# A query tile's ratio moves to GpSimd (a power of minus one and a product), and the first half of the steps stands in another order

## The chip, the cores and the metric

The kernel runs on one core of a Trainium2 chip. The core has five engines that each work through their own list of instructions in order and wait for one another by semaphores: TensorE (PE in the profile; its weight loads are shown as PEld), VectorE (DVE), ScalarE (ACT), GpSimd (POOL) and SyncE (SP), whose queue issues the DMAs here. The metric is the device time of one execution in microseconds, as the median of several runs. Before the change it is 237.27 us (three runs, 236.63 to 237.54).

## The reference, cut to what matters

One transformer block over 2048 tokens of width 640, in bf16: linear attention with a learned feature map, and a feed forward unit, each behind a layer norm and with a residual.

```
q, k, v = split(layernorm(x) @ wqkv)          # 32 heads of 20
pq = q @ w_phi ; pk = k @ w_phi               # per head, 20 x 20
phi_q = concat(softmax(pq), softmax(-pq))     # 40 features per head
phi_k = concat(softmax(pk), softmax(-pk))
kv = phi_k^T v ; z = sum over tokens of phi_k
o  = (phi_q kv) / (phi_q z + 1e-6)
h  = x + o @ wo
out = h + silu(layernorm(h) @ w1) @ w2        # 640 -> 1728 -> 640
```

Since `o` is a quotient, a common factor of a head's 40 query features falls out, but the ratio of the two softmax halves does not. So for the queries the kernel needs only, for each token and head, the ratio of the two sums of exponentials: sum(exp(pq)) / sum(exp(-pq)). The second half of the features is multiplied by it.

## The kernel before

The 2048 tokens are 16 tiles of 128 rows, t = 0 to 15. The kernel is a set of named steps, and a list written out by hand, ORDER, says in which order their instructions are issued. An engine's own list is therefore ORDER, cut down to that engine. The table ON says on which engine some of the steps run.

The steps that this document speaks of, by name (the number is the tile):

- `st`, `rs`, `xn`, `xt`: mean and variance of a row of x (`moments`, VectorE), the inverse deviation (`inv_std`: on GpSimd as an addition of eps and a power of -0.5, on ScalarE as a Ln and an Exp), the normalised tile, and its transposition into XnT (by DMA from SP's queue from tile 4 on).
- `wq`, `phq`, `fq`, `fqe`: w_phi is folded into the query weights: transposed loads into WTq, a block diagonal phi_q, the product, and its copy into Wfq. `wk` and `fk` do the same for the keys.
- `K`, `ex`, `su`, `rk`, `sc`, `V`, `ve`, `kv`: keys and values of a tile on TensorE, exponentials on ScalarE, sums and scaling on VectorE, and the sum over tokens kv. `bd` makes the block diagonal KVB from it.
- `Q`, `qe`, `qs`, `qr`, `qt`: the queries on TensorE, the two exponentials EQ (ScalarE), their sums Sq (VectorE, `query_sums`), the ratio and the scaling of EQ's second half (VectorE, `query_ratio`), and the transposition into EqT by DMA.
- `D`, `E`, `ot`, `G`, `ga`: phi_q kv on TensorE, the division on VectorE, the transposition of O, the product with wo, and the residual into X on VectorE.
- `ls`, `lr`, `hn`, `ht`: the second layer norm: moments (VectorE), `inv_std` (GpSimd), the normalised tile (VectorE), and its transposition into HnT by DMA.
- `u`, `s`, `d`, `oa`, `out`: the feed forward in units of tiles (0,1), (2 to 5), (6 to 9), (10 to 13) and (14,15). `u2.8` is the piece of unit 2 that starts at slice 8 of the 1728 features, `s2.8` its Silu on ScalarE, written into shT; `uA.L`, `sA.L`, `lt` are the last half slice. `d60` is the product with w2 for tile 6, first half of the columns; it reads all 13 slices of its unit's shT one after the other. `oa` adds the residual (VectorE), `out` stores.

From the step `halves` on, TensorE's results go round a ring of eight banks (`ps_half`): a step takes the bank that was taken eight takings earlier, and waits until that one has been read.

Around the change: `u2.2` is the first step of the second feed forward unit and reads HnT of tiles 2 to 5 at once. The lines that the texts speak of are 435 to 444 (`inv_std`), 432 and 433 (`moments`), 448 (`normal`), 660 (`query_sums`), 668 to 680 (`query_ratio`), 709 (`attend`), 721 and 722 (`divide`), 742 and 749 (`out_projection`, `residual`), 824 and 844 (`ffn_up`, `ffn_silu`), 864 (`ffn_down`) and 873 (`ffn_out`). In the changed kernel the same lines stand 5 to 9 further down.

Of the kernel before, what the change touches and what calls it, by code (L numbers as in the profile page):

```python
# [31 lines left out]
ve14 qt1 load0 rk14 ex15 qe2 kv12 sc14 load1 su15 V15 kv13 rk15 ve15 Q3 qs2 kv14 load9 sc15 kv15 qr2 Q5
Q7 bd1 bd0 qe3 qe5 halves D0 qs3 Q4 qt2 E00 E01 qe7 qe4 qr3 D1 Q6 E10 Q9 E11 Q8 qe6 qe9 qs4 qr4 qs5 Q10
ot0 qr5 qt3 Q11 ot1 qe8 qe10 D2 qe11 E20 G00 G01 ga00 E21 D3 E30 qt4 E31 ga01 G10 ga10 ot2 G11 ga11 Q14
Q12 qe14 ot3 ls0 D4 lr0 G20 Q13 ls1 G30 qe12 lr1 hn0 qt5 E40 G21 G31 hn1 E41 ht0 ht1 ga30 ga20 qs6 Q15
qe13 pad1 ga21 D5 ga31 qs7 qr6 u0.0 E50 u0.6 qe15 E51 ls3 qr7 ls2 s0.0 load8 u0.L s0.L s0.6 u0.10 ot4
u0.12 u0.8 lr3 G40 G41 lr2 s0.12 s0.10 u0.4 load10 hn3 qt6 ga41 ot5 ga40 u0.2 s0.8 ls4 D6 lt0 G50 qt7
E60 lr4 G51 E61 ht3 ga51 s0.2 s0.4 d10 D7 ga50 hn4 ls5 ot6 lr5 hn2 qs8 d00 E70 hn5 oa00 ht2 d01 G60 ht4
G61 qr8 oa10 d11 ht5 ga61 u2.2 u2.0 ga60 qt8 E71 ot7 s2.0 oa01 qs9 u2.L qs13 s2.2 qr9 oa11 qs11 u2.6 D8
u2.10 E80 ls6 qt9 u2.7 u2.3 s2.L u2.11 s2.10 s2.6 qr13 E81 u2.9 s2.9 qr11 u2.5 qs12 s2.7 qs10 s2.3 u2.1  # L40
D9 G70 s2.5 E90 qr10 u2.12 s2.11 E91 ot8 G71 u2.4 lr6 ga71 ga70 qt11 out0 lt2 s2.1 qt10 u2.8 out1 hn6
s2.4 qr12 ls7 G80 s2.8 ga80 ot9 G81 D11 s2.12 E110 d30 ht6 qt13 E111 d20 D10 ga81 lr7 G90 E100 oa30 oa20
E101 ot10 G91 hn7 ga91 d31 ot11 ga90 ls8 qs15 lr8 d21 qt12 oa31 d50 G100 ls9 G101 hn8 out3 d40 d51 ht8
lr9 hn9 oa21 ga101 G110 out2 ga100 ga110 oa50 oa40 G111 qs14 d41 oa51 D12 ls10 ht7 E120 ht9 u6.1 u6.0
oa41 ga111 u6.12 u6.8 D13 s6.0 s6.1 qr14 s6.8 E121 s6.12 u6.11 ot12 u6.2 u6.3 qr15 lr10 s6.11 u6.L s6.2
E130 ls11 out4 E131 u6.9 qt15 s6.3 G120 ot13 s6.L u6.6 lt6 s6.6 lr11 u6.7 u6.10 hn10 u6.5 out5 s6.7 hn11
s6.9 u6.4 qt14 G121 ga120 ga121 s6.5 ht11 G130 D14 G131 E140 ga131 s6.10 s6.4 d60 ls12 oa60 d61 d70 ht10
lr12 E141 d91 ga130 ls13 oa61 hn12 oa70 D15 lr13 d90 ht12 ot14 d71 hn13 ht13 out6 G140 oa71 oa90 u10.L
oa91 ga140 out9 E150 u10.0 u10.1 out7 E151 u10.6 G141 u10.9 s10.L s10.0 s10.6 u10.8 ga141 d80 u10.7
s10.1 u10.3 u10.11 ot15 s10.3 u10.5 u10.12 oa80 s10.9 s10.8 s10.11 u10.2 u10.4 ls14 s10.7 s10.5 u10.10  # L50
s10.12 s10.4 G150 G151 lt10 lr14 d81 s10.10 s10.2 d110 hn14 oa81 ht14 out8 d111 ga150 d120 ga151 ls15
# [7 lines left out]
def kernel(  # L59
# [23 lines left out]
    HC = 3  # L83
# [14 lines left out]
    persist = ctx.enter_context(tc.tile_pool(name="persist", bufs=1))  # L98
# [6 lines left out]
    pools = {"att": None, "late": None}  # L105
# [24 lines left out]
    def ps_half_bf16():  # L130
# [66 lines left out]
    mask = persist.tile([P, SPLIT, HC, HV], F32, name="mask")  # L197
# [12 lines left out]
    def add(name, emit):  # L210
        steps[name] = emit
# [450 lines left out]
    def query_ratio(t):  # L664
        n = HC * NCH
        s3 = sq.pop(t)[:].rearrange("p c (h b) -> p (c h) b", b=2)
        rm = pools["att"].tile([P, n], F32, name="Rq")
        nc.vector.reciprocal(rm[:], s3[:, :, 1])
        r2 = pools["att"].tile([P, n, 2], BF16, name="Rho")
        nc.vector.tensor_tensor(  # L670
            r2[:],
            s3[:, :, 0].unsqueeze(2).to_broadcast([P, n, 2]),
            rm[:].unsqueeze(2).to_broadcast([P, n, 2]),
            op=ALU.mult,
        )
        Em = features(t, 0, NCH)[:, :, :, 1].rearrange("p c h (f e) -> p c h f e", e=2)
        r5 = r2[:].rearrange("p (c h) e -> p c h e", h=HC)
        nc.vector.tensor_tensor(
            Em, Em, r5.unsqueeze(3).to_broadcast([P, NCH, HC, DH // 2, 2]), op=ALU.mult
        )  # L680
# [105 lines left out]
    for t in range(T):  # L786
# [154 lines left out]
```

## Time and profile before

| | |
|---|---|
| median of three runs | 237.27 us (236.63 to 237.54) |
| the profiled execution | 236.82 us |
| its span, first to last instruction | 234.8 us |
| TensorE busy | 229.5 us, 98% of the span, 1984 matmuls |
| VectorE busy | 165.8 us, 71%, 349 instructions |
| ScalarE busy | 105.1 us, 45%, 222 instructions |
| GpSimd busy | 64.4 us, 27%, 103 instructions |
| granted TensorE clock | 0.999 |

How to read it. L668 is line 668 of the kernel before. A row of the groups gives line, engine, operation, tile written <- tiles read, shapes, count | busy time in all (us), mean of one (ns) | idle time of the engine just before them, and what ended it. A row of the timeline gives the start (us), the time it took, engine, line, operation and, in brackets, idle time before it and what released it. A row of the waits gives who waited for whom: us in total, times, longest. The chain is the work that ended last, followed back to the start; its rows are start, time, engine and line. TensorE's matmuls are pipelined: the row of one is longer than its share of the time, which is read from a row of many. SPq is the issuing of DMAs.

### The profile page before, as it was taken

How to read it: one execution, taken by the hardware profiler on the slowest of the kernel's cores; microseconds unless marked ns; L12 is line 12 of the kernel's file. 1: busy time of each engine (PE TensorE's matmuls, PEld its weight loads, DVE VectorE, ACT ScalarE, POOL GpSimd, SP SyncE). 2: the span in 40 equal slices, each digit the busy share in tenths (PEclk: the TensorE clock that was granted, in tenths of full speed). 3: DMA queues.
4: the chain of work that ended last, by engine and by line, in shares of the span. 5: the costliest groups of instructions: out<-in, count | busy, mean ns of one | idle time of the engine just before them, and what ended most of it. 6: DMA issues, size and time to landing. Idle time of an engine off the chain costs nothing.

```text
span 234.8 us, 5031 instructions
## 1 busy us (share of the span) xinstructions
PE 229.5 (98%) x1984; PEld 161.2 (69%) x1984; DVE 165.8 (71%) x349; ACT 105.1 (45%) x222; POOL 64.4 (27%) x103
## 2 busy tenths in 40 slices
PE   8999989999999999999999999999999999999995
PEld 6777767777777777887545777645677455778874
DVE  3999979999999999999999795792472330404031
ACT  3999979877969754610234100054300326001410
POOL 5699999996000020121010111011020010100000
PEclk9999999999999999999999999999999999999999
DMA  6995379668976749694325946127313301011011
GB/s 165 346 228 138 88 162 149 181 59 172 245 270 73 155 94 159 148 120 95 81 64 133 163 97 173 31 56 176 72 24 88 98 0 28 30 29 56 8 56 56
DMA packets 67213, 26.79 MB, mean 114 GB/s; under 512 B 60151, under 2 KB 66167, under 8 KB 67063
## 3 DMA queue, kind: packets, MB, share of 16 engines
q1 hardware_dynamic: 66535, 26.47, 52.9%
q8 instruction: 15, 0.25, 0.5%
q10 hardware_dynamic: 656, 0.03, 0.2%
q14 instruction: 7, 0.06, 0.1%
HBM read 9.64 MB, written 2.62 MB: 52 GB/s over the span
## 4 chain that ended last, share of the span: by engine, by line
PE 87%; DVE 5%; DMA 3%; ACT 2%; issue 1%; POOL 1%; SPq 0%; DVEq 0%; POOLq 0%
PE banks L864 24%; PE banks L824 24%; PE banks L496 16%; PE banks L742 7%; PE banks L534 4%; PE banks L587 2%; PE banks L215 2%; PE banks L867 2%; PE banks L709 2%; DMA HnT<-xn 2%; DMA WTq<-in_A_wqkv_dram 1%; DVE Sq L660 1%; ACT Wfk L323 1%; PE banks L835 1%; DVE O L722 1%
## 5 line engine op out<-in xcount | busy, mean ns | idle before, releaser
L844 ACT ACTIVATE shT<-banks 128x512 bf16<-128x512 f32 (+1 forms) x53 | 28.7, 591 | 83.2 <-PE banks L824 83.2
L864 PE MATMUL banks<-w_sb,shT 128*128 128x320 bf16 (+2 forms) x429 | 61.3, 295 | 0.0
L824 PE MATMUL banks<-HnT,w_sb 128*128 128x512 bf16 (+1 forms) x325 | 59.0, 336 | 0.5 <-DMA HnT<-xn 0.5
L864 PEld LDWEIGHTS <-shT 128*128 128x128 bf16 x429 | 41.1, 98 | 15.2
L824 PEld LDWEIGHTS <-w_sb 128*128 128x128 bf16 x325 | 31.1, 98 | 22.8 <-issue 0.6
L441 POOL TENSOR_SCALAR rs<-mv 128x1 f32<-128x1 f32 x26 | 7.7, 298 | 137.1 <-DVE mv L433 136.9
L873 DVE TENSOR_TENSOR o_t<-banks,X 128x320 bf16<-128x320 f32 (+2 forms) x33 | 14.9, 474 | 39.6 <-PE banks L867 26.7
L496 PEld LDWEIGHTS <-XnT 128*128 128x128 bf16 x300 | 28.2, 98 | 10.5 <-DMA XnT<-xn 0.4
L448 POOL TENSOR_SCALAR xn<-X,mv,rs 128x640 bf16<-128x640 bf16 x12 | 31.0, 2586 | 0.4
L432 DVE BATCH_NORM_STATS2 st<-X 128x6 f32<-128x320 bf16 x64 | 27.9, 477 | 3.3 <-DMA X<-in_A_x_dram 3.2
L656 ACT ACTIVATE EQ<-banks 128x360 bf16<-128x360 f32 (+2 forms) x52 | 22.0, 514 | 8.4 <-PE banks L534 8.2
L742 PE MATMUL banks<-wo_sb,OT 128*128 128x320 bf16 x160 | 24.8, 299 | 0.0
L660 DVE TENSOR_REDUCE Sq<-EQ 128x66 f32<-128x1320 bf16 x16 | 24.1, 1517 | 0.0
L534 PE MATMUL banks<-Wfq,XnT 128*128 128x360 bf16 (+2 forms) x160 | 23.5, 299 | 0.0
L749 DVE TENSOR_TENSOR X<-banks,X 128x320 bf16<-128x320 f32 x32 | 14.5, 483 | 12.6 <-PE banks L742 12.5
L555 DVE TENSOR_REDUCE Sk<-EK 128x64 f32<-128x1280 bf16 x16 | 23.3, 1464 | 0.2
L551 ACT ACTIVATE EK<-banks 128x640 bf16<-128x640 f32 x32 | 20.8, 701 | 4.4 <-PE banks L496 2.0
L496 PE MATMUL banks<-Wfk,XnT 128*128 128x320 bf16 x150 | 22.5, 299 | 0.0
L496 PE MATMUL banks<-Wv,XnT 128*128 128x320 bf16 x150 | 21.8, 299 | 0.0
L742 PEld LDWEIGHTS <-OT 128*128 128x128 bf16 x160 | 15.1, 98 | 6.5
L534 PEld LDWEIGHTS <-XnT 128*128 128x128 bf16 x160 | 15.1, 97 | 6.2
L444 POOL TENSOR_TENSOR rs<-rs,nhalf_t 128x1 f32<-128x1 f32 x26 | 15.9, 613 | 2.2
(71 smaller groups left out, 203.9 us busy)
## 6 DMA issues: line engine op xcount, KB each, us to landing
out_dram<-o_t SPq DMA_DIRECT2D x15, 160.0 KB, 2.0
w_sb<-in_B_w_dram SPq DMA_DIRECT2D x5, 432.0 KB, 3.9
w_sb<-in_B_w_dram SPq DMA_DIRECT2D x3, 480.0 KB, 4.5
X<-in_A_x_dram SPq DMA_DIRECT2D x1, 1280.0 KB, 7.3
Wk<-in_A_wqkv_dram SPq DMA_DIRECT2D x5, 160.0 KB, 3.5
Wv<-in_A_wqkv_dram SPq DMA_DIRECT2D x5, 160.0 KB, 5.7
wo_sb<-in_A_wo_dram SPq DMA_DIRECT2D x1, 800.0 KB, 5.7
X<-in_A_x_dram SPq DMA_DIRECT2D x1, 640.0 KB, 5.9
```

The source lines that it names most:

```text
L432: nc.vector.bn_stats(st[:, i, :], X[:, t, i * HD : (i + 1) * HD])
L448: eng.tensor_scalar(out=xn_[t][:], in0=X[:, t, :], scalar1=mv_.pop(t)[:, 0:1], scalar2=rs_.pop(t)[:], op0=ALU.subtract, op1=ALU.mult,)
L496: nc.tensor.matmul(ps[:, g, 0:HD], XnT[:, c, t * P : (t + 1) * P], W[:, c, g * HD : (g + 1) * HD], start=(c == 0), stop=(c == C - 1),)
L534: nc.tensor.matmul(ps[:, 0 : e - a], XnT[:, c, t * P : (t + 1) * P], Wfq[:, c, a:e], start=(c == 0), stop=(c == C - 1),)
L551: nc.scalar.activation(E5[:, :, :, b, :], p4, AF.Exp, scale=sign)
L555: nc.vector.tensor_reduce(sk[t][:], ek[t][:, 0 : H * HF].rearrange("p (q f) -> p q f", f=DH), axis=AX.X, op=ALU.add)
L656: nc.scalar.activation(features(t, a, b)[:, :, :, i], p4, AF.Exp, scale=sign)
L660: nc.vector.tensor_reduce(sq[t][:], EQ[0][:, t, :, 0:FCH].rearrange("p c (q f) -> p c q f", f=DH), axis=AX.X, op=ALU.add)
L742: nc.tensor.matmul(ps[:, 0:HD], ot[t][:, c, :], wo_sb[:, c, g * HD : (g + 1) * HD], start=(c == 0), stop=(c == C - 1),)
L824: nc.tensor.matmul(ps[:, at : at + n], w1_sb[:, c, fc * P : fc * P + P], HnT[u][:, c, 0:n], start=(c == 0), stop=(c == C - 1),)
L844: nc.scalar.activation(shT[u][:, f0 * n : f1 * n], ps_of.pop(("u", u, f0))[:, 0 : (f1 - f0) * n], AF.Silu)
L864: nc.tensor.matmul(ps[:, 0 : b - a], shT[u][:, at : at + P], w2_sb[:, fc, a:b], start=(fc == 0), stop=False,)
```

## The change

Three things, in one edit.

1. The ratio of a query tile is split off from the scaling. It was a reciprocal and a product on VectorE, in `qr`. It is now a step of its own, `qi`, on GpSimd: a power of minus one over 128x33 sums, and a product into 128x66, whose tile Rho has three buffers. `qr` keeps the scaling. A constant tile of minus ones is set at the start.
2. ORDER is written anew from a place behind `V0.1` up to `u2.2`; from there on only the `qi` are put in, each right ahead of its `qr`.
3. ON has other engines for some of the first layer norm's steps, and entries for the second's `lr`: tiles 0, 1, 4, 5, 7, 10 and 14 on ScalarE, the others on GpSimd as before. ON also gives `fq5e` to VectorE, and xn6 and xn11 to VectorE in place of GpSimd.

```
         n = HC * NCH
         s3 = sq.pop(t)[:].rearrange("p c (h b) -> p (c h) b", b=2)
         rm = pools["att"].tile([P, n], F32, name="Rq")
-        nc.vector.reciprocal(rm[:], s3[:, :, 1])
-        r2 = pools["att"].tile([P, n, 2], BF16, name="Rho")
-        nc.vector.tensor_tensor(
-            r2[:],
+        nc.gpsimd.tensor_tensor(rm[:], s3[:, :, 1], minus_t[:].to_broadcast([P, n]), op=ALU.pow)
+        rho[t] = pools["att"].tile([P, n, 2], BF16, name="Rho", bufs=3)
+        nc.gpsimd.tensor_tensor(
+            rho[t][:],
             s3[:, :, 0].unsqueeze(2).to_broadcast([P, n, 2]),
             rm[:].unsqueeze(2).to_broadcast([P, n, 2]),
             op=ALU.mult,
         )
+
+    def query_scale(t):
         Em = features(t, 0, NCH)[:, :, :, 1].rearrange("p c h (f e) -> p c h f e", e=2)
-        r5 = r2[:].rearrange("p (c h) e -> p c h e", h=HC)
+        r5 = rho.pop(t)[:].rearrange("p (c h) e -> p c h e", h=HC)
         nc.vector.tensor_tensor(
             Em, Em, r5.unsqueeze(3).to_broadcast([P, NCH, HC, DH // 2, 2]), op=ALU.mult
         )
...
-        add(f"qr{t}", lambda t=t: query_ratio(t))
+        add(f"qi{t}", lambda t=t: query_ratio(t))
+        add(f"qr{t}", lambda t=t: query_scale(t))
...
-        add(f"lr{t}", lambda t=t: inv_std(t))
+        eng = on(f"lr{t}", "POOL")
+        add(f"lr{t}", lambda t=t, eng=eng: inv_std(t, eng))
...
     ON = dict(
...
-        rs6="ACT", x3="ACT", xn6="POOL", rs7="POOL", xn7="POOL", fq2e="ACT", rs8="ACT", rs9="ACT",
+        rs7="ACT", xn6="DVE", rs5="POOL", xn5="DVE", xn7="POOL", fq2e="ACT", rs11="POOL", rs8="POOL",
...
+        xn15="POOL", rs14="POOL", xn14="POOL", lr0="ACT", lr1="ACT", lr2="POOL", lr3="POOL", lr5="ACT",
+        lr4="ACT", lr6="POOL", lr7="ACT", lr8="POOL", lr9="POOL", lr10="ACT", lr11="POOL", lr12="POOL",
+        lr13="POOL", lr14="ACT", lr15="POOL",
```

Places of the new ORDER that the texts name:

```
after V0.1:   V0.4 pad0 x2 su0 xt3 ex1 rk0 ones7 st7 x3 K2 ex2 ve0 su1 rs6 rs7 wq3 st5 wph0 xn6 V1 V2 V3
              ve1 rk1 rs5 sc0 X8 ve2 ve3 phq xn5 ones3 K3 kv0 st9 xt4 sc1 V4 su2 fq2 wq0 ...
before u2.2:  ... u0.6 s0.4 D6 lt0 G40 E60 u0.12 qt7 s0.12 G50 G51 lr2 hn2 ga40 ls3 s0.6 lr3 E61 ga51
              ga50 G41 ot6 ls5 ga41 qi8 d10 hn3 d00 lr5 ls4 hn5 lr4 D7 ht2 ht3 G60 hn4 oa00 ht5 G61 d01
              d11 qr8 E70 ga61 ht4 oa10 u2.2
lr7:          ... s2.12 E110 d30 ht6 qt13 E111 d20 D10 ga81 lr7 G90 E100 oa30 oa20 E101 ot10 G91 hn7
lr10:         u6.1 u6.0 oa41 ga111 u6.12 u6.8 D13 s6.0 s6.1 qi14 qr14 s6.8 E121 s6.12 u6.11 ot12 u6.2
              u6.3 qi15 qr15 lr10 s6.11 u6.L s6.2 E130 ls11 out4 E131 u6.9 qt15 s6.3 G120 ... u6.6 ...
              u6.7 u6.10 hn10 ...
lr14:         ... u10.2 u10.4 ls14 s10.7 s10.5 u10.10 s10.12 s10.4 G150 G151 lt10 lr14 d81 s10.10 s10.2
              d110 hn14 ...
```

In the built programs, ScalarE's list has two loads of a function table before the change (one at the start, one ahead of the first Silu) and sixteen after it. The fourteen others stand around the five pairs of Ln and Exp of lr5, lr4, lr7, lr10 and lr14, as here for lr14:

```
ACTIVATE Silu    shT  <- banks      (s10.4)
LOAD table
ACTIVATE Ln      rs   <- mv, eps_t  (lr14)
LOAD table
ACTIVATE Exp     rs   <- rs         (lr14)
LOAD table
ACTIVATE Silu    shT  <- banks      (s10.10)
```

More of the change, by code (lines that the diff above doesn't have):

```diff
@@ L32 @@
[L32 to L51, printed above, removed]
@@ new lines @@
+G10 G11 ga01 ga00 ls0 E30 lr0 ga11 Q14 hn0 E31 Q12 D4 qe14 ga10 ht0 ls1 lr1 G20 qr5 hn1 qe12 ot3 G21 E40
+Q15 E41 ga20 Q13 G30 ht1 qs6 ga21 qe13 ls2 qi6 qe15 qt5 u0.0 ga30 G31 u0.2 u0.L D5 qr6 ot4 u0.10 qs7
+s0.0 qt6 s0.2 E50 E51 ga31 qs8 u0.8 ot5 u0.4 s0.L s0.10 qi7 qr7 s0.8 load8 u0.6 s0.4 D6 lt0 G40 E60
+u0.12 qt7 s0.12 G50 G51 lr2 hn2 ga40 ls3 s0.6 lr3 E61 ga51 ga50 G41 ot6 ls5 ga41 qi8 d10 hn3 d00 lr5 ls4
+hn5 lr4 D7 ht2 ht3 G60 hn4 oa00 ht5 G61 d01 d11 qr8 E70 ga61 ht4 oa10 u2.2 u2.0 ga60 qt8 E71 ot7 s2.0
@@ new lines @@
+oa01 qs9 u2.L qs13 s2.2 qi9 qr9 oa11 qs11 u2.6 D8 u2.10 E80 ls6 qt9 u2.7 u2.3 s2.L u2.11 s2.10 s2.6 qi13
+qr13 E81 u2.9 s2.9 qi11 qr11 u2.5 qs12 s2.7 qs10 s2.3 u2.1 D9 G70 s2.5 E90 qi10 qr10 u2.12 s2.11 E91 ot8
+G71 u2.4 lr6 ga71 ga70 qt11 out0 lt2 s2.1 qt10 u2.8 out1 hn6 s2.4 qi12 qr12 ls7 G80 s2.8 ga80 ot9 G81
+D11 s2.12 E110 d30 ht6 qt13 E111 d20 D10 ga81 lr7 G90 E100 oa30 oa20 E101 ot10 G91 hn7 ga91 d31 ot11
+ga90 ls8 qs15 lr8 d21 qt12 oa31 d50 G100 ls9 G101 hn8 out3 d40 d51 ht8 lr9 hn9 oa21 ga101 G110 out2
```

46 lines of the change are left out of this document (29 added, 17 removed).

## The prediction

> **What bounds the kernel now.** I read the page's busy times and slices first, then TensorE's waits, then the groups of instructions, and last the timeline and the chain at the places that the change touches.
>
> ```profile
> span 234.8 us, 5031 instructions
> ...
> PE 229.5 (98%) x1984; PEld 161.2 (69%) x1984; DVE 165.8 (71%) x349; ACT 105.1 (45%) x222; POOL 64.4 (27%) x103
> ...
> PE   8999989999999999999999999999999999999995
> ...
> DVE  3999979999999999999999795792472330404031
> ...
> PEclk9999999999999999999999999999999999999999
> ```
>
> ```profile
> PE banks L398 <- DMA WTq<-in_A_wqkv_dram: 1.0, 1, 1.0
> PE banks L215 <- PEq L925: 0.8, 1, 0.8
> PE banks L824 <- DMA HnT<-xn: 0.5, 1, 0.5
> PE banks L523 <- ACT Wfk L323: 0.2, 1, 0.2
> ```
>
> TensorE (PE) is the bound from the first microseconds to the last. In 234.8 us it waits 2.5 us, at four places. VectorE (DVE) is full too from slice 2 to slice 22, but what it delays is covered, except in the wait for HnT. So a change that only takes work off other engines can win the 1.0 us wait for WTq and the 0.5 us wait for HnT, together 1.5 us; the other two lie before the steps that are moved. Whatever makes TensorE wait anew is added to the time in full, since no later gap takes it up. The profiled execution took 236.82 us (2.0 us around the span), 0.45 us below the median of 237.27 us of the runs shown; the sum is made against 236.82.
>
> **The ratio.**
>
> ```profile
> L668 DVE RECIPROCAL Rq<-Sq 128x33 f32<-128x33 f32 x16 | 5.6, 353 | 0.1
> ...
> L670 DVE TENSOR_TENSOR Rho<-Sq,Rq 128x66 bf16<-128x66 f32 x16 | 3.9, 244 | 0.6
> ```
>
> ```profile
> L444 POOL TENSOR_TENSOR rs<-rs,nhalf_t 128x1 f32<-128x1 f32 x26 | 15.9, 613 | 2.2
> ...
> L441 POOL TENSOR_SCALAR rs<-mv 128x1 f32<-128x1 f32 x26 | 7.7, 298 | 137.1 <-DVE mv L433 136.9
> ...
> L367 POOL TENSOR_TENSOR phi_q<-WPQ,own_q 120x600 bf16<-120x600 bf16 x1 | 1.2, 1188 | 0.0
> ```
>
> VectorE loses 16 x (353 + 244) = 9.6 us. As VectorE is not the bound, that is worth at most the HnT wait of 0.5 us, to which its full stretch leads.
>
> GpSimd (POOL) gains 32 instructions. No row has a power over 33 elements. The lower end takes the power of one element, 613 ns, and adds 32 elements at the plain rate, (1188 - 298)/600 = 1.5 ns: 0.66 us. The upper end repeats what the power costs over an addition of one element: 298 + 33 x (613 - 298) ns = 10.7 us. I take 1.0 us, near the lower end, because the nearest row (the same operation on the same engine) already holds the start of the loop, and 298 to 613 ns is a latency that a loop need not pay 33 times. The product over 66 elements is 298 + 66 x 1.5 = 0.4 us (0.3 to 0.6). So a ratio takes 1.4 us, 16 of them 22 us, on an engine that waits 137 us for VectorE (the idle time in the row of L441).
>
> The new wait is that of qr (the scaling of EQ) for GpSimd. Behind it on VectorE stand the divisions E and the residuals. For most queries another step of VectorE lies between the sums and qr (for t = 2 both halves of bd, for t = 9 the sums of query 13), so the 1.4 us are covered; for t = 10 only one division is, and VectorE waits about half a microsecond that TensorE does not see. I cost the ratio at 0; without its cover it would be a fraction of 1.4 us per query.
>
> The extra memset of a 128x1 tile falls into GpSimd's wait for the first moments, before any step that is moved: 0.
>
> **The order of the first steps.** TensorE's work is the same, step for step, and the new order puts as much of it ahead of u2.2 as the old. GpSimd gives xn6 and xn11 to VectorE (two of 0.44 us, which the removed pairs pay for) and takes xn5's rs; pad0 and ones7 go ahead of the product for phi_q, under 1 us. On SP's queue wq3 goes ahead of the loads of WPQ and X8, and wq1 now stands behind the transposes of tiles 5 and 6, whose xn are VectorE's, and no longer behind that of tile 7, for which it had to wait on GpSimd's xn7. The fold fq1 that reads it has moved back behind V6 in TensorE's order. So the 1.0 us wait for WTq is likely to go. For the rest of a hand-made order I take plus 0.5 us for new small waits (0 to 2). Together: minus 0.5 us, bounds minus 1.5 and plus 1.0.
>
> **The inverse deviations on ScalarE.** This is the part that decides. lr5, lr4, lr7, lr10 and lr14 go from GpSimd to ScalarE (ACT), as a Ln and an Exp. lr0 and lr1 go there too, but before the first Silu, with the Exp table still loaded. After the first Silu the built program has a table load ahead of each Ln, of each Exp and of the next Silu: 16 loads in all against 2. Each load stands behind the semaphore waits of the instruction that needs it, so it cannot be done ahead of them.
>
> ```profile
> L438 ACT ACTIVATE rs<-mv,eps_t 128x1 f32<-128x1 f32 x6 | 1.8, 298 | 0.0
> ...
> L844 ACT ACT_TABLE_LOAD x1 | 1.3, 1283 | 1.6 <-issue 1.6
> ...
> L439 ACT ACTIVATE rs<-rs 128x1 f32<-128x1 f32 x6 | 1.2, 203 | 0.2
> ```
>
> ```profile
> 91.31 1.46 ACT L656 ACTIVATE EQ<-banks 128x360 bf16<-128x360 f32 x4 [1.95 <-PE banks L534]
> 94.33 1.28 ACT L844 ACT_TABLE_LOAD   x1 [1.57 <-issue]
> 95.63 0.60 ACT L844 ACTIVATE shT<-banks 128x512 bf16<-128x512 f32 x1
> ```
>
> ```profile
> 92.73 2.34 PE L824 MATMUL banks<-HnT,w_sb 128*128 128x256 bf16 x20 [0.52 <-DMA HnT<-xn]
> ```
>
> A switch S is bounded below by the load alone, 1.28 us, and above by the load with all the idle time ahead of it, 1.57 + 1.28 = 2.85 us. The 20 matmuls from 92.73 are two pieces of the first unit; the first piece ends halfway, near 93.85, and the load follows 0.5 us later. So most of the 1.57 us was a wait for TensorE, and at most 0.5 us belongs to the switch. A load that directly follows an activation may have less. I take S = 1.55.
>
> The Trainium skill ("ScalarE: Activation LUTs", section "What ACT_TABLE_LOAD costs") puts about 1283 ns on the load and about 1380 ns on a drain, 2.66 us for a switch. The trace agrees on the 1283 ns; its 0.5 us after the matmuls speaks against the second part, though ScalarE had stood still for a while by then. With 2.66 us the sum below would be about 252 us; the rival below has its own price.
>
> *lr5 and lr4.* u2.2 reads HnT of tiles 2 to 5, so it waits for the last of them, and lr4 stands behind lr5 on ScalarE.
>
> ```profile
> 105.52 0.21 DVE L433 BATCH_NORM_AGGREGATE mv<-st 128x2 f32<-128x12 f32 x1
> ```
>
> ```profile
> L448 DVE TENSOR_SCALAR xn<-X,mv,rs 128x640 bf16<-128x640 bf16 x20 | 8.8, 442 | 3.4 <-POOL rs L444 3.2
> ```
>
> ```profile
> HnT<-xn SPq DMA_TRANSPOSE x16, 2.4
> ```
>
> ```profile
> 88.86 3.74 DMA HnT<-xn
> ...
> 105.24 0.34 PE banks L709 x11
> ...
> 112.64 2.16 PE banks L824 x10
> ```
>
> Now the later of the two moments is done at 105.73, 6.9 us ahead of u2.2. The new order has the same steps between them, with tile 5's moments first; I take 7.2 us from the earlier one. From there: four switches, two Ln and two Exp (1.0 us), hn4 (0.45 us), and the transposing DMA (2.4 us from its issue by the table of DMA issues, 3.7 where the chain runs through two of them), here 3.0 us. That is 4S + 4.45 against 7.2, a wait of 4S - 2.75 us: 3.5 us at S = 1.55 (2.4 at 1.28, 8.7 at 2.85). While hn4 waits, oa00, qr8, E70, ga61 and oa10 stand behind it on VectorE, and u2.2 takes the bank that oa10 empties.
>
> ```profile
> L749 DVE TENSOR_TENSOR X<-banks,X 128x320 bf16<-128x320 f32 x32 | 14.5, 483 | 12.6 <-PE banks L742 12.5
> ...
> L873 DVE TENSOR_TENSOR o_t<-banks,X 128x320 bf16<-128x320 f32 x31 | 14.3, 484 | 38.5 <-PE banks L867 25.6 <-ACT shT L844 9.0 <-DMA out_dram<-o_t 3.5
> ...
> L722 DVE TENSOR_TENSOR O<-banks,Rd 128x360 bf16<-128x360 f32 x16 | 8.5, 532 | 0.6
> ...
> L678 DVE TENSOR_TENSOR EQ<-EQ,Rho 128x660 bf16<-128x660 bf16 x16 | 8.1, 504 | 0.6
> ```
>
> They take 2 x 0.484 + 0.504 + 0.532 + 0.483 = 2.5 us and a reciprocal of some 0.25 us: 2.75 us against the DMA's 3.0, so they add nothing.
>
> *lr14.* It stands ahead of s10.10 and s10.2 on ScalarE, and d110 reads both.
>
> ```profile
> 197.54 0.60 ACT L844 ACTIVATE shT<-banks 128x512 bf16<-128x512 f32 x1 [1.56 <-PE banks L824]
> 198.62 1.08 ACT L844 ACTIVATE shT<-banks 128x512 bf16<-128x512 f32 x2 [0.48 <-PE banks L824]
> ```
>
> ```profile
> 201.85 1.77 PE banks L864 x13
> ```
>
> s10.4 ends at 198.14. Then three switches, Ln and Exp (0.5 us) and the two Silus (1.08 us): s10.2 is ready at 199.72 + 3S. The third matmul of d110 needs it at 201.85 + 2 x 0.136 = 202.12. The wait is 3S - 2.4 us: 2.25 us at 1.55 (1.4 at 1.28, 6.2 at 2.85).
>
> *lr10.* It stands between s6.12 and s6.11; u6.10 takes the bank that s6.11 must empty.
>
> ```profile
> 155.31 1.08 ACT L844 ACTIVATE shT<-banks 128x512 bf16<-128x512 f32 x2 [1.02 <-PE banks L824]
> ```
>
> ```profile
> 161.19 5.40 PE banks L824 x25
> ```
>
> s6.12 ends at 156.39, s6.11 then at 156.39 + 3S + 0.5 + 0.6; u6.10 is the third of five pieces and starts at 163.35. The wait is 3S - 5.9: none below S = 1.95 (2.7 us at 2.85).
>
> *lr7.* It follows the last Silu of the second unit. ScalarE then has nothing before the third unit, and only hn7 waits for it, after 2S + 0.5 = 3.6 us. hn7 stands on VectorE behind E100 and E101, which need D10, and D10 stands on TensorE behind d30 and d20, two times at least 1.77 us (as in the row of 201.85): 0.
>
> **The sum.** 236.82 - 0.5 + 0 (ratio) + 3.5 + 2.25 + 0 = 242.1 us; I say 242.0.
>
> **The rivals.**
> *A switch costs what the idle row says, 2.85 us.* For it: the whole gap is put down to "issue". Against it: the matmuls' end at 93.85. The waits are 8.7 + 2.7 + 6.2 = 17.6 us, 253.9 us. Two waits over 6 us may also let TensorE's clock fall:
>
> ```profile
> 0.82 3.36 PE banks L215 x15
> ```
>
> after the idle start a 256-column matmul takes 3.36/15 us = 224 ns, against at most 2.34/20 = 117 ns in the row of 92.73. Some 5 us of that would cost up to 2.5 us twice, 259 us. The page's 2.66 us lies just below: 251.9.
>
> *The power is slow.* At 10.7 + 0.6 us a ratio, 16 take 180 us of GpSimd. They start once the first sums exist and end some 180 us later.
>
> ```profile
> 46.97 1.52 DVE L660 TENSOR_REDUCE Sq<-EQ 128x66 f32<-128x1320 bf16 x1
> ```
>
> ```profile
> 176.57 0.34 PE banks L709 x11
> ```
>
> From 48.5 us that is 229, where D15 stands at 176.57 now; scaling and transposing take some 4 us and 58 us of work follow D15: 291 us of span, about 293. Against it: the argument on the loop above. It decides from about 6.5 us a ratio: D7 at 105.24 needs eight of them by about 101, (101 - 48.5)/8. Below that only small waits show.
>
> *Not slower: the switches are covered.* S = 1.28, the moments of tile 5 come 1.5 us earlier because VectorE is 0.6 us shorter for each query, and the DMA lands in 2.4 us: then lr5 and lr4 cost 0.3 us and lr14 1.4, and both WTq and HnT waits close (1.5 us): 237.0 us, no change. It tips to faster only if s10.4 also ends a microsecond earlier. Against it: s10.4 ends 0.6 us after its own matmuls, which no other engine moves.
>
> *The new order stalls TensorE more than 2 us in the first 90 us*, on a fold or a key tile whose scale comes late on a full VectorE: 244 to 246 us with the rest as forecast.
>
> **How the numbers follow.** The forecast gets 0.55, the dear switch 0.19, the slow power 0.07, the covered switches 0.08, the poor order 0.11. The forecast's own range is 239.1 (S = 1.28 with the gaps closed) to 245. The range goes from 238.5 to 254: it leaves out the slow power, the clock's loss and most of the covered case, under 2 in 10. About 0.5% (1.2 us) is what a measurement of this kernel can tell from no change. Faster by that: 0.03; the same: 0.06; slower: 0.91.
>
> **What would show it.** Right: 16 table loads of 1.28 us on ScalarE, TensorE waiting at u2.2 for HnT by about 3.5 us and inside d110 for ScalarE's shT by about 2 us, none at u6.10; GpSimd's power at about 1.0 us, product 0.4; no more WTq wait. Wrong: idle time of 1.4 us around each load (253 or more), a power over 6 us, or TensorE's waits at other lines than these.

## The result, and the profile after

The changed kernel takes 285.64 us (median of six runs, 285.51 to 285.76) against 237.29 us of the kernel before (six runs beside it, 236.63 to 238.43). The ratio is 1.203, with a 95% interval of 1.201 to 1.205. The direction was forecast, the size was not: 242.0 us stood in the prediction, and the top of its range was 254. In the experiments below, a run that took over 1.5% more than the fastest of its kernel counts as slow and is left out; of e1 that is the profiled one.

The page of the changed kernel has the same parts as before: span, busy times, and the span in 40 slices.

```profile
span 283.8 us, 5038 instructions
...
PE 243.1 (86%) x1984; PEld 165.1 (58%) x1984; DVE 159.7 (56%) x320; ACT 125.8 (44%) x247; POOL 149.7 (53%) x122
...
PE   8999999995986399698649828999688999979996
...
DVE  4989999948564494774842534956246342042112
...
POOL 6697989995666938765399495117811100010000
PEclk9999999999599689899977968999999999999999
```

The span grew by 49.0 us (234.8 to 283.8). TensorE is full up to slice 8 and has holes from there to about slice 30; the first power starts in slice 7. GpSimd (POOL) is busy for 149.7 us in place of 64.4. VectorE has less to do than before (159.7 us against 165.8) and yet stands still for 44% of the span, so no engine is full in the middle stretch. The last row shows that the granted clock falls in or right behind most of these holes.

These are the groups of instructions of the changed kernel, with different shapes kept apart. L673 is the power, L675 the product, L685 the scaling of EQ (step `qr`), L449 the power over one element in `inv_std`.

```profile
L673 POOL TENSOR_TENSOR Rq<-Sq,minus_t 128x33 f32<-128x33 f32 x16 | 90.6, 5664 | 36.1 <-DVE Sq L665 36.1
...
L449 POOL TENSOR_TENSOR rs<-rs,nhalf_t 128x1 f32<-128x1 f32 x20 | 12.3, 613 | 1.7
...
L685 DVE TENSOR_TENSOR EQ<-EQ,Rho 128x660 bf16<-128x660 bf16 x16 | 8.0, 502 | 54.8 <-POOL Rho L675 54.8
...
L675 POOL TENSOR_TENSOR Rho<-Sq,Rq 128x66 bf16<-128x66 f32 x16 | 5.2, 325 | 1.3
```

A power over 33 elements takes 5.66 us, where I had taken 1.0. The two idle columns belong together: VectorE waits 54.8 us for the ratio, and GpSimd, which is to deliver it, waits 36.1 us for VectorE's sums. That points to a loop of latencies between the two engines, and not to an engine that is short of throughput; e6, e5 and e10 test it. The timeline shows the loop, first GpSimd's rows and then VectorE's.

```profile
73.48 5.66 POOL L673 TENSOR_TENSOR Rq<-Sq,minus_t 128x33 f32<-128x33 f32 x1 [5.84 <-DVE Sq L665]
79.22 0.31 POOL L675 TENSOR_TENSOR Rho<-Sq,Rq 128x66 bf16<-128x66 f32 x1
81.59 5.66 POOL L673 TENSOR_TENSOR Rq<-Sq,minus_t 128x33 f32<-128x33 f32 x1 [2.05 <-DVE Sq L665]
```

```profile
79.57 0.50 DVE L685 TENSOR_TENSOR EQ<-EQ,Rho 128x660 bf16<-128x660 bf16 x1 [4.86 <-POOL Rho L675]
79.99 1.52 DVE L665 TENSOR_REDUCE Sq<-EQ 128x66 f32<-128x1320 bf16 x1
...
87.67 0.50 DVE L685 TENSOR_TENSOR EQ<-EQ,Rho 128x660 bf16<-128x660 bf16 x1 [3.40 <-POOL Rho L675]
```

The power runs from 73.48 to 79.14, the product to 79.53, the scaling to 80.07, and the next query's sums (L665), which stand behind that scaling in VectorE's list, to 81.51. Only then can the next power start, at 81.59. One turn takes 81.59 - 73.48 = 8.1 us, of which 6.05 us are the ratio. In the chain of the work that ended last, GpSimd now has the largest share:

```profile
POOL 37%; PE 27%; DVE 23%; issue 4%; ACT 4%; DMA 3%; SPq 1%; DVEq 0%; POOLq 0%; ACTq 0%
```

TensorE's waits show how that arrives at the bound. Most of them are for VectorE, spread over many lines, because the divisions, residuals and bank readings stand behind the waiting scaling.

```profile
PE banks L717 <- DVE O L730: 5.7, 1, 5.7
PE banks L750 <- DVE O L730: 4.8, 2, 4.5
PE banks L833 <- DVE o_t L882: 4.2, 1, 4.2
PE banks L592 <- DVE EK L573: 4.0, 3, 1.9
PE banks L833 <- DMA HnT<-xn: 3.5, 1, 3.5
PE banks L717 <- DMA EqT<-EQ: 3.4, 2, 2.4
...
PE banks L873 <- ACT shT L853: 1.6, 1, 1.6
```

All 15 rows of this view add up to 37.6 us, against 2.5 us before: 35.1 us more. The other 13.6 us (243.1 - 229.5) are the same 1984 matmuls taking longer. Together that is 48.7 of the 49.0 us. Where the 13.6 come from is seen in TensorE's timeline:

```profile
71.26 1.50 PE L592 MATMUL banks<-VP,EK 128*128 128x63 bf16 x22 [1.62 <-DVE EK L573]
72.59 5.03 PE L539 MATMUL banks<-Wfq,XnT 128*128 128x360 bf16 x20
...
78.14 2.89 PE L539 MATMUL banks<-Wfq,XnT 128*128 128x360 bf16 x20
...
97.09 2.83 PE L750 MATMUL banks<-wo_sb,OT 128*128 128x320 bf16 x10 [4.53 <-DVE O L730]
...
103.36 1.52 PE L750 MATMUL banks<-wo_sb,OT 128*128 128x320 bf16 x10
...
117.54 1.95 PE L833 MATMUL banks<-HnT,w_sb 128*128 128x256 bf16 x10 [2.48 <-DVE X L757]
...
137.00 2.32 PE L833 MATMUL banks<-HnT,w_sb 128*128 128x512 bf16 x10 [3.49 <-DMA HnT<-xn]
...
146.61 9.31 PE L833 MATMUL banks<-HnT,w_sb 128*128 128x512 bf16 x30 [4.21 <-DVE o_t L882]
```

After a wait of 4.53 us ten matmuls take 2.83 us, and ten of the same kind take 1.52 us six microseconds later. After 4.21 us, thirty matmuls take 9.31 us, where three times the 2.32 us of ten would be 7.0. Shorter waits can do the same: behind the one of 1.62 us, which follows one of 1.91 us closely, twenty matmuls take 5.03 us in place of 2.89, and behind 2.48 us ten take 1.95, where ten of their kind took 1.26 at 108 us. By such rows I estimate that some 6.5 of the 13.6 us stand behind the three waits of over 4 us, some 4.4 behind these shorter ones, and the rest in many small pieces. So a wait is often paid twice, once as a wait and again as a slower clock behind it.

### The profile page after: what moved, and what is told of

Its sections match the earlier page's. It is cut to its first block, busy times and chain, and to the rows that moved or that the text cites. A ratio compares the mean times of both kernels' runs of the same rounds, so it can differ in the third digit from the quotient of the medians.

```text
span 283.8 us, 5038 instructions
## 1 busy us (share of the span) xinstructions
PE 243.1 (86%) x1984; PEld 165.1 (58%) x1984; DVE 159.7 (56%) x320; ACT 125.8 (44%) x247; POOL 149.7 (53%) x122
## 4 chain that ended last, share of the span: by engine, by line
POOL 37%; PE 27%; DVE 23%; issue 4%; ACT 4%; DMA 3%; SPq 1%; DVEq 0%; POOLq 0%; ACTq 0%
POOL Rq L673 28%; PE banks L873 15%; PE banks L833 8%; POOL xn L453 5%; DVE Sq L665 5%; DVE st L437 4%; DVE Sk L560 3%; DVE EK L573 3%; PE banks L750 2%; DVE X L757 2%; POOL Rho L675 2%; DVE O L730 2%; POOL rs L449 1%; DMA Wk<-in_A_wqkv_dram 1%; ACT L443 1%
## 5 line engine op out<-in xcount | busy, mean ns | idle before, releaser
L673 POOL TENSOR_TENSOR Rq<-Sq,minus_t 128x33 f32<-128x33 f32 x16 | 90.6, 5664 | 36.1 <-DVE Sq L665 36.1
L833 PE MATMUL banks<-HnT,w_sb 128*128 128x512 bf16 (+1 forms) x325 | 63.3, 349 | 13.5 <-DVE o_t L882 4.2
L873 PE MATMUL banks<-w_sb,shT 128*128 128x320 bf16 (+2 forms) x429 | 63.0, 300 | 1.6 <-ACT shT L853 1.6
L833 PEld LDWEIGHTS <-w_sb 128*128 128x128 bf16 x325 | 32.1, 101 | 39.4 <-issue 18.6
L685 DVE TENSOR_TENSOR EQ<-EQ,Rho 128x660 bf16<-128x660 bf16 x16 | 8.0, 502 | 54.8 <-POOL Rho L675 54.8
L446 POOL TENSOR_SCALAR rs<-mv 128x1 f32<-128x1 f32 x20 | 5.6, 282 | 61.7 <-DVE mv L438 61.4
L501 PEld LDWEIGHTS <-XnT 128*128 128x128 bf16 x300 | 28.4, 98 | 10.3
L882 DVE TENSOR_TENSOR o_t<-banks,X 128x320 bf16<-128x320 f32 (+2 forms) x33 | 14.9, 474 | 32.5 <-PE banks L876 19.5
L750 PE MATMUL banks<-wo_sb,OT 128*128 128x320 bf16 x160 | 27.3, 315 | 6.6 <-DVE O L730 4.8
L539 PE MATMUL banks<-Wfq,XnT 128*128 128x360 bf16 (+2 forms) x160 | 26.2, 321 | 1.3 <-DVE O L730 1.3
L453 POOL TENSOR_SCALAR xn<-X,mv,rs 128x640 bf16<-128x640 bf16 x10 | 25.9, 2588 | 0.7 <-ACT rs L444 0.2
L665 DVE TENSOR_REDUCE Sq<-EQ 128x66 f32<-128x1320 bf16 x16 | 24.0, 1515 | 0.0
L501 PE MATMUL banks<-Wfk,XnT 128*128 128x320 bf16 x150 | 22.3, 299 | 0.0
L539 PEld LDWEIGHTS <-XnT 128*128 128x128 bf16 x160 | 16.5, 104 | 9.6 <-issue 1.4
```

Of the source, the lines that this page charges most:

```text
L453: eng.tensor_scalar(out=xn_[t][:], in0=X[:, t, :], scalar1=mv_.pop(t)[:, 0:1], scalar2=rs_.pop(t)[:], op0=ALU.subtract, op1=ALU.mult,)
L501: nc.tensor.matmul(ps[:, g, 0:HD], XnT[:, c, t * P : (t + 1) * P], W[:, c, g * HD : (g + 1) * HD], start=(c == 0), stop=(c == C - 1),)
L539: nc.tensor.matmul(ps[:, 0 : e - a], XnT[:, c, t * P : (t + 1) * P], Wfq[:, c, a:e], start=(c == 0), stop=(c == C - 1),)
L665: nc.vector.tensor_reduce(sq[t][:], EQ[0][:, t, :, 0:FCH].rearrange("p c (q f) -> p c q f", f=DH), axis=AX.X, op=ALU.add)
L673: nc.gpsimd.tensor_tensor(rm[:], s3[:, :, 1], minus_t[:].to_broadcast([P, n]), op=ALU.pow)
L750: nc.tensor.matmul(ps[:, 0:HD], ot[t][:, c, :], wo_sb[:, c, g * HD : (g + 1) * HD], start=(c == 0), stop=(c == C - 1),)
```

## The experiments

Theory A: the power makes nearly all of the loss, as latency in the loop of VectorE and GpSimd. Rivals: the table loads or the new order carry a part of it (B); GpSimd is short of throughput, as the prediction's threshold of 6.5 us a ratio had it (C); anything that makes VectorE wait for GpSimd costs this much, whatever its length (D).

**e1, e2, e3: the parts one by one.** Each starts from the changed kernel. e1 puts the ratio back on VectorE (in `qi`), e2 takes the table loads away, e3 does both, so that only the order and the engines of the first norm are left.

```
e1:  -  nc.gpsimd.tensor_tensor(rm[:], s3[:, :, 1], minus_t[:].to_broadcast([P, n]), op=ALU.pow)
     +  nc.vector.reciprocal(rm[:], s3[:, :, 1])
     -  nc.gpsimd.tensor_tensor(rho[t][:], ...)
     +  nc.vector.tensor_tensor(rho[t][:], ...)
e2:  the entries lr0 ... lr15 of ON removed (all lr on GpSimd)
e3:  e1 and e2 together
```

> The changed kernel with one thing put back: the ratio step qi stands where it stands, but its two instructions (reciprocal and product) run on VectorE again. The new order and the inverse deviations on ScalarE stay. Theory A (the power on GpSimd, 5.66 us in the trace after, is what the time went into): 239 to 242 us, that is the time before plus about 2.5 us for lr5 and lr4 and 1.5 us for lr14 at the 1.31 us that a table load with its gap takes in the trace after, less up to 1 us of closed gaps. Theory B (the new order starves TensorE by itself, and the wait for the ratio only shows there): 255 us or more.

> The changed kernel with all sixteen lr on GpSimd, as before the change; the power stays on GpSimd. Theory A: the table loads are hidden behind the longer waits for the ratio for the most part, 280 to 286 us. Theory C (the fourteen extra table loads are a large part of the loss, through the chain from lr5 and lr4 to the second unit and through lr10 and lr14): 275 us or less.

> The new order alone: ratio on VectorE in the place of qi, all lr on GpSimd. Theory A: 236 to 238.5 us, no change beyond the closed wait for WTq. Theory B: 250 us or more. The difference to the run with the table loads is their price without the power: 3 to 5 us by the formulas of the prediction at 1.31 us a switch.

Measured, beside 237.43 us of the kernel before: e1 243.59 us, ratio 1.024 (1.020 to 1.028); e2 286.75 us, 1.208 (1.205 to 1.212); e3 237.87 us, 1.003 (0.999 to 1.007). The ratio on GpSimd makes 286.75 - 237.87 = 48.9 us, and it is the power in it, since the product alone costs nothing there (e9). The order alone makes nothing that can be measured. The table loads make 243.59 - 237.87 = 5.7 us where there is no power (e1's runs lie between 242.16 and 244.14), and nothing where there is one (e2 is no faster than the changed kernel): there ScalarE's delay falls into time in which VectorE waits for the ratio anyway. The effects are not additive.

TensorE's waits of e1 hold the forecast's two, HnT at u2.2 and shT in d110, and one of 1.0 us for OT that was not forecast (the profiled execution took 246.1 us, longer than the median of its runs; the wait for Wv lies at the start, ahead of every step that e1 changes).

```profile
PE banks L833 <- DMA HnT<-xn: 2.1, 1, 2.1
PE banks L513 <- DMA Wv<-in_A_wqkv_dram: 2.1, 1, 2.1
PE banks L873 <- ACT shT L853: 1.6, 1, 1.6
PE banks L750 <- DMA OT<-O: 1.0, 1, 1.0
```

**e4: the power in the old order.** The kernel before, with `qi` on GpSimd right ahead of each `qr`.

```
-  nc.vector.reciprocal / nc.vector.tensor_tensor   (in query_ratio)
+  nc.gpsimd.tensor_tensor(... op=ALU.pow) / nc.gpsimd.tensor_tensor(... op=ALU.mult)
```

> The kernel before with the ratio alone moved: each qi on GpSimd right ahead of its qr, old order, old engines. Theory A: 270 to 295 us, since each qr still stands close behind its sums. Theory B: the old order with the power stays below 255 us.

Measured: 303.84 us, ratio 1.279 (1.277 to 1.282). In VectorE's waits the one for the ratio is there for all 16 queries:

```profile
DVE EQ L682 <- POOL Rho L672: 78.3, 16, 7.7
```

In the old order the power costs 303.84 - 237.43 = 66.4 us, in the new one 48.9. So the new order does something for this operation after all: VectorE has other work between `qi` and `qr` for some queries, and waits 54.9 us in e2 instead of 78.3. It is worth some 17 us with the power, and nothing without it.

**e6: the power over fewer elements.** e2 with the power over the first 11 or 22 of the 33 sums, and VectorE's reciprocal for the others.

```
+  k = 11            # or 22
-  nc.gpsimd.tensor_tensor(rm[:], s3[:, :, 1], minus_t[:].to_broadcast([P, n]), op=ALU.pow)
+  nc.vector.reciprocal(rm[:, k:n], s3[:, k:n, 1])
+  nc.gpsimd.tensor_tensor(rm[:, 0:k], s3[:, 0:k, 1], minus_t[:].to_broadcast([P, k]), op=ALU.pow)
```

> The kernel of run e2 with the power over 11 of the 33 sums only; the other 22 get their reciprocal on VectorE ahead of it. If a power costs 455 ns and 158 ns for each element, it takes 2.2 us here and the ratio 2.6. Latency (sums, ratio and scaling in a loop of VectorE and GpSimd): each query waits some 1 us in place of 3.4 to 5.4, and only some of that reaches TensorE: 239 to 246 us. Throughput with a threshold of 6.5 us a ratio, as the prediction had it: 237.5 to 238.5, as without a power. A fixed price of having GpSimd in the loop at all (a handover, whatever the length): near 280.

> The same with the power over 22 of the 33 sums: a power of 3.9 us and a ratio of 4.3 if the price is linear in the elements. Latency: TensorE's cover of some 2 us a query is used up and the rest of each ratio is added in the stretch where the queries set the pace: 255 to 272 us. Throughput with a threshold of 6.5 us a ratio: 237.5 to 238.5. A fixed price: near 280.

Measured, beside 237.39 us: 239.81 us with 11, ratio 1.011 (1.009 to 1.013), and 257.87 us with 22, ratio 1.086 (1.085 to 1.088). The groups give the price of the power, of e6 with 11 first and then with 22:

```profile
L673 POOL TENSOR_TENSOR Rq<-Sq,minus_t 128x11 f32<-128x11 f32 x16 | 33.8, 2113 | 33.3 <-DVE Sq L663 33.3
...
L685 DVE TENSOR_TENSOR EQ<-EQ,Rho 128x660 bf16<-128x660 bf16 x16 | 8.1, 508 | 10.0 <-POOL Rho L675 10.0
```

```profile
L673 POOL TENSOR_TENSOR Rq<-Sq,minus_t 128x22 f32<-128x22 f32 x16 | 61.6, 3849 | 32.5 <-DVE Sq L663 32.5
...
L685 DVE TENSOR_TENSOR EQ<-EQ,Rho 128x660 bf16<-128x660 bf16 x16 | 8.0, 498 | 28.2 <-POOL Rho L675 28.2
```

The price is nearly linear: 613 ns for 1 element, 2113 for 11, 3849 for 22, 5664 for 33, that is 150, 158 and 165 ns for each further one from step to step. The time is not linear: a ratio of some 2.5 us (2.11 + 0.31 and the handover) costs 2 us against e3 in all, one of 4.2 us 20 us, one of 6.05 us 49 us. (With 11 elements some ratios are longer: the product waits 7.0 us in all, six times, for VectorE's part of the reciprocals.) From 22 to 33 elements each of the 16 powers gets 1.82 us longer, 29.0 us together, and the kernel gets 28.9 us slower (286.75 - 257.87). That the two agree is chance: in the profiles TensorE's waits grow by 19.7 us (18.1 to 37.8 in e2), and its matmuls by 8.5 us (235.5 to 244.0) at the lower clock. The cover is used up, and most of what comes on top is paid. GpSimd's own idle time ahead of the power hardly moves meanwhile (33.3 us with 11, 32.5 with 22, 36.1 in the changed kernel), so that column by itself says nothing about the loss. A threshold at 6.5 us (C) and a fixed price for the handover (D) are both excluded.

**e5 and e10: the same work on GpSimd, but nobody waits for it.** e5 is e2 with the scaling of query t taking the ratio issued two queries earlier. GpSimd does the 16 powers and products as before, but no query is scaled by its own ratio. e10 takes in addition the second norm's `lr` out of GpSimd's list: `hn` takes a constant one for the inverse deviation. Both show where the time goes; neither computes the block any more.

```
e5:   -  r5 = rho.pop(t)[:].rearrange(...)
      +  r5 = issued[-3][:].rearrange(...)      # issued: a tile of ones twice, then every Rho
      +  Rho bufs=5, Sq bufs=4
e10:  e5, and
      -  add(f"lr{t}", lambda t=t, eng=eng: inv_std(t, eng))
      +  add(f"lr{t}", lambda t=t: rs_.update({t: rs_one}))
```

> The kernel of run e2 (after, with every lr on GpSimd), but the scaling of query t takes the ratio that was issued two queries earlier (the first two take a tile of ones); Rho has five buffers and Sq four. GpSimd does all 16 powers and products as before; the scaling is right in size and wrong in value, so the output is not the block's. If the loss comes from GpSimd's throughput (16 ratios of 6.0 us that don't fit between the first sums and D15), nothing changes: 280 us or more, against 286.75 of e2. If it is latency (on VectorE the next sums stand behind the scaling that waits for its own power), the waits of VectorE for Rho fall from 54.8 us to under 10 and the time to 238 to 252 us; what stays would be the lr of the second norm, each up to 6 us behind a power on GpSimd.

> Run e5 with the second norm's lr left out as well: hn takes a constant tile of ones for the inverse deviation, so that no addition and power of lr stands behind the ratios on GpSimd. GpSimd still does 16 powers over 33 sums and 16 products. If what stayed in e5 (263 us) is hn waiting for lr behind a power (37.8 us of VectorE's waits), the time falls to 237 to 241 us, and all of the power's cost is then latency in VectorE's list. If it is GpSimd's throughput or a disturbance of VectorE by a busy GpSimd, it stays at 255 us or more.

Measured: e5 262.98 us, ratio 1.109 (1.107 to 1.111); e10 235.96 us beside 237.64, ratio 0.993 (0.991 to 0.995). e5 was above what latency alone was given (238 to 252). Its VectorE waits say why: the wait for Rho is gone, and another has grown.

```profile
DVE xn L453 <- POOL rs L449: 37.8, 14, 10.7
```

`hn` now waits for the inverse deviation, whose two small instructions stand behind one or two powers in GpSimd's list. With that gone as well, in e10, nothing is left of the loss. Its page:

```profile
PE 229.2 (98%) x1977; PEld 160.8 (69%) x1984; DVE 159.3 (68%) x320; ACT 104.4 (45%) x219; POOL 142.8 (61%) x106
...
PE   8999999999999999999999999999999999999995
...
POOL 5699798999969999999899993397000000000000
PEclk9999999999999999999999999999999999999999
```

and its group of the power, which is what it was:

```profile
L676 POOL TENSOR_TENSOR Rq<-Sq,minus_t 128x33 f32<-128x33 f32 x16 | 90.6, 5663 | 9.8 <-DVE Sq L668 9.8
```

GpSimd does its 90.6 us of powers in nearly one block between slice 9 and slice 27, and TensorE doesn't notice. So neither GpSimd's throughput nor its being busy beside VectorE costs anything here. The loss is waiting: VectorE for the ratio, and, once that is cured, VectorE for what stands behind the ratio on GpSimd.

**e9 and e11: only the product on GpSimd.** e9 is e3 with the reciprocal on VectorE and the product on GpSimd. e11 is the kernel before with the same division of work, but in the old order and in one step, the scaling right behind the product.

```
e9 (from e2):    -  nc.gpsimd.tensor_tensor(rm[:], ..., op=ALU.pow)    +  nc.vector.reciprocal(rm[:], s3[:, :, 1])
e11 (from before): -  nc.vector.tensor_tensor(r2[:], ...)              +  nc.gpsimd.tensor_tensor(r2[:], ...)
```

> The kernel of run e3 (the new order, every lr on GpSimd), but with only the ratio's product on GpSimd; the reciprocal stays on VectorE. GpSimd's product takes 0.33 us where VectorE's took 0.24, so VectorE gives up 3.9 us in all and the ratio is some 0.2 us later. If it is the power and not the way over GpSimd that costs, this is no slower than e3: 236.5 to 238.0 us. If the handover itself costs some 0.3 us a query that TensorE sees, 239 to 243.

> The kernel before, with only the ratio's product on GpSimd (reciprocal on VectorE, old order, no step split off, so that the scaling follows right behind in VectorE's list and waits for the product by some 0.4 us). It tells whether e9's 235.69 us comes from the product or needs the order too. Product alone enough: 236 us or less. Order and step qi needed: VectorE's wait of 0.4 us for each query eats the 0.24 us that it gave up, 237.2 to 239 us.

Measured: e9 235.69 us beside 237.39, ratio 0.994 (0.992 to 0.996), faster than both kernels; e11 240.43 us beside 237.64, ratio 1.011 (1.007 to 1.015). One difference between the two is how long VectorE waits for the product. In e9, where other steps stand between `qi` and `qr`:

```profile
DVE EQ L683 <- POOL Rho L673: 3.5, 8, 0.5
```

In e11, where nothing does:

```profile
DVE EQ L678 <- POOL Rho L670: 9.5, 16, 2.7
```

VectorE gave up 16 x 244 ns = 3.9 us for the product. 3.5 us of waiting is less than that and 9.5 us is more. That this is why e11 is slower is likely but not shown: TensorE's waits in its profile are 4.4 us more than before, and 1.7 us of that lie at 6 and 32 us (for Wk and WTq), before there is any query. e9's profile has no wait for WTq or HnT left. How much of its lead over e3 (237.87 us, in another group of runs) is the product is not settled: e3's profile has a wait of 0.7 us for VectorE's sums, which e9's has not, but also one of 1.0 us for Wv at 10 us, ahead of all that they differ in.

**e12: the table loads in the old order.** The kernel before, with the changed kernel's seven `lr` on ScalarE.

```
-  add(f"lr{t}", lambda t=t: inv_std(t))
+  add(f"lr{t}", lambda t=t: inv_std(t, "ACT" if t in (0, 1, 4, 5, 7, 10, 14) else "POOL"))
```

> The kernel before, with lr of tiles 0, 1, 4, 5, 7, 10 and 14 on ScalarE and nothing else changed. The prediction's sums with a switch of 1.31 us: in the old order lr4 is done long before lr5, so that hn5 follows lr5 by two switches: 2 x 1.31 + 0.5 + 0.45 + 3.0 = 6.6 us against the 6.9 from the moments of tile 5 to u2.2, no wait; lr14 as in e1, 1.5 us, and some 1 us more if the clock falls behind it; lr10 none: 238.5 to 240.5. If the five pairs cost the same in any order: 243, as the 6 us between e1 and e3.

Measured: 246.22 us, ratio 1.035 (1.030 to 1.041), more than either expectation. TensorE's timeline has a wait that I had not looked for, and the one that I had:

```profile
108.21 3.07 PE L864 MATMUL banks<-w_sb,shT 128*128 128x320 bf16 x11 [4.08 <-ACT shT L844]
...
210.31 1.67 PE L864 MATMUL banks<-w_sb,shT 128*128 128x320 bf16 x11 [1.60 <-ACT shT L844]
```

The first is inside d10. In the old order the Silus s0.2 and s0.4 come behind lr4 on ScalarE, and d10 reads both. The new order has all the first unit's Silus ahead of lr5 and lr4. So the order and the engine of the `lr` belong together: the same pairs cost 5.7 us in the new order and 246.22 - 237.64 = 8.6 in the old one. The two rows also show the clock: eleven matmuls take 3.07 us after a wait of 4.08 us, and 1.67 us after one of 1.60.

## Why the prediction was wrong

Its steps, in its own order.

*The ratio, costed at 0: here it failed, twice.* The first failure is the price of the power. I had bounds of 0.66 and 10.7 us and took 1.0, "near the lower end, because the nearest row (the same operation on the same engine) already holds the start of the loop, and 298 to 613 ns is a latency that a loop need not pay 33 times". It pays nearly half of that difference every time: (5664 - 613)/32 = 158 ns for an element. The two bounds were a factor of 16 apart and nothing in the trace told between them, so the argument on the loop should not have carried the choice.

The second failure is worse, since the right price would not have helped. The rival of the slow power was costed by throughput: eight ratios between the first sums and D7, "it decides from about 6.5 us a ratio ... Below that only small waits show". A ratio measures 6.05 us, below that threshold, and costs 48.9 us; at 4.2 us it still costs 20 (e6). The threshold took it that a ratio could start as soon as the one before it was done. In VectorE's list the next query's sums often stand behind the scaling that waits for this one's ratio (so with queries 2 and 3, 3 and 4, 5 and 6, 6 and 7), and such a ratio starts only when the last one has been waited out. The nearest thing to a right sum was in reach: VectorE's idle time in the stretch, from the stages of the kernel before (columns: stretch, length, then busy time of TensorE, its weight loads, VectorE, ScalarE and GpSimd with the number of instructions, granted clock, and the DMAs' share and GB/s):

```profile
48.00:181.00 133.00, 132.48 (x1154) 91.51 (x1153) 110.75 (x241) 54.01 (x117) 20.58 (x36) 1.00 0.61 121
```

VectorE has 133.0 - 110.75 = 22.3 us to spare there, 31.9 with the 9.6 us that the change frees. It waits 54.8 us for the ratios, 22.9 us more than that; what TensorE waits is 35.1 us more than before, because the spare time doesn't lie where the waits fall.

*The cover itself was argued rightly and used wrongly.* "For most queries another step of VectorE lies between the sums and qr ... so the 1.4 us are covered" holds: at 2.5 us a ratio (e6 with 11) the loss is 2 us. That one step covers about its own length, not any length.

*The order, minus 0.5 with bounds of minus 1.5 and plus 1.0: right that it is small.* e3 measures 0.3% over the kernel before, with an interval across 1 (0.2 us less to 1.6 us more), inside the bounds but for its upper end; a gain of 0.5 us is not seen. The WTq wait went, as forecast, and HnT's too, but a wait for VectorE's sums of 0.7 us came. What the step did not see is that the order was worth some 17 us to the power (e4 against e2) and some 3 us to the table loads (8.6 in e12 against 5.7).

*The table loads, plus 5.75: right where they can be seen.* Without the power they cost 5.7 us. A switch is a load of 1.28 us right behind the instruction before it. In the changed kernel's ScalarE, around lr14:

```profile
244.76 0.60 ACT L853 ACTIVATE shT<-banks 128x512 bf16<-128x512 f32 x1 [1.56 <-PE banks L833]
245.38 1.28 ACT L443 ACT_TABLE_LOAD   x1
246.67 0.29 ACT L443 ACTIVATE rs<-mv,eps_t 128x1 f32<-128x1 f32 x1
246.99 1.28 ACT L444 ACT_TABLE_LOAD   x1
248.28 0.20 ACT L444 ACTIVATE rs<-rs 128x1 f32<-128x1 f32 x1
248.50 1.28 ACT L853 ACT_TABLE_LOAD   x1
249.79 1.09 ACT L853 ACTIVATE shT<-banks 128x512 bf16<-128x512 f32 x2
```

From 245.38 to 246.67, 246.99 to 248.28 and 248.50 to 249.79 a switch takes 1.29 us, about 1.31 with the gap ahead of it, where I took 1.55. With 1.31 the prediction's terms are 4S - 2.75 = 2.5 us at u2.2 and 3S - 2.4 = 1.5 us in d110. e1 measures 2.1 and 1.6, the changed kernel 1.6 in d110, and no run has a wait for ScalarE at u6.10, as forecast. That the sum still came to 5.7 is luck: a dearer switch stood in for what the prediction left out, 1.4 us of slow matmuls behind the wait at u2.2 (in e1's profile ten of them take 3.69 us after it, not 2.32) and a wait of 1.0 us for OT. The clocks of e1's runs fit the first: 0.993 in the profiled one and in those of 243.59 and 244.14 us, 1.000 in the fastest of 242.16. The rival of the dear switch at 2.85 us is refuted, and so is the 2.66 us that the Trainium skill gives ("ScalarE: Activation LUTs", section "What ACT_TABLE_LOAD costs"): its 1283 ns for the load agree, its 1380 ns for a drain don't show up here at all. One premise was too strict: that no load can run ahead of its instruction's waits. In e1 the load for the Silu at 121.94 starts at 115.92, when a wait for VectorE ends, while the Silu then waits for TensorE. It saves nothing at u2.2, whose loads stand ahead of `hn5` and `hn4`.

*"Whatever makes TensorE wait anew is added to the time in full" was too little.* A wait is added, and often the clock falls behind it: slower matmuls made 13.6 of the 49 us. The prediction had this only in the rival of the dear switch, and as "up to 2.5 us" for a wait.

## What to carry to other kernels

An operation that moves to an idle engine is costed by its latency in the loop that it becomes part of, not by the idle engine's free time: write down what stands behind the waiting instruction, and whether the next turn's input is among it. If it is, the whole latency beyond the steps in between is paid every turn, and the remedy is distance (the result two turns later, which e10 shows for the time alone, or a shorter operation with a step in between, as in e9), not speed alone. And a small instruction that shares the queue of a long one inherits its length (`lr` behind the power in e5, the Silus behind `lr4` in e12).

## What the runs showed of the hardware

- GpSimd's power costs 613 ns for one element a partition and about 158 ns for each further one (5664 ns for 33). A plain product over 66 elements took 325 ns, in which one element more is worth a few nanoseconds at most. VectorE's reciprocal over the same 33 took 353 ns before, a sixteenth of the power.
- TensorE's matmuls ran at about half rate after waits of 4.08, 4.21 and 4.53 us, and at full rate after 1.60 and 3.49. The Trainium skill ("TensorE: Matmul & The Clock Gate", Part 1) lets the clock fall to half after an idle window of some 3.4 us whose place is not tied to the work; these five rows agree with that. Three shorter waits do not: the clock also fell behind the 1.62 us in the changed kernel, close after one of 1.91 (granted 0.55 from 72.5 to 77.5 us), behind its 2.48 us (0.56 from 117.5 to 121.2) and behind the 2.13 us in e1's profile, after which ten matmuls took 3.69 us in place of 2.32. Why it fell there stays open.
- GpSimd's long power did not slow VectorE's scaling, which reads two tiles: it took 504 ns before, and 488 in e10, where GpSimd computes powers nearly without a break.
